# Linear attention into a sine-gated MLP on one core: a new first stage, w_in's first block in four DMAs, a re-planned order

## The chip, the cores and the metric

The kernel runs on one core of a Trainium2 chip, as one program. The core has five engines that run their own instruction streams and meet at semaphores: TensorE (PE, its weight loads shown apart as PEld), VectorE (DVE), ScalarE (ACT), GpSimd (POOL) and SyncE (SP). Data come from HBM by DMAs that POOL, ACT and SP issue. The metric is device time in microseconds (us) of one execution; a kernel's time is the median of several.

## The reference, cut to what matters

Two stages. Linear attention with a decay per head (4 batches, 8 heads, 768 tokens, head size 64), in blocks of tokens:

```
intra = (q_b k_b^T * Dmask) v_b          Dmask[i,j] = lam_h^(i-j) for i >= j, else 0
out_b = intra + (q_b * lam^(pos+1)) S    S: the carried state of the head, 64 x 64
S     = lam^block * S + (k_b * lam^(block-1-pos))^T v_b
```

Its output, laid out as x [3072 tokens, 512], goes through

```
h = x @ w_in            w_in  [512, 2048]
g = h + sin(alpha*h)^2 / alpha
y = g @ w_out           w_out [2048, 512], y is float32
```

## The kernel before, in words

**Tiling.** The reference's block of 64 tokens is computed in chunks of 128 tokens (the recurrence allows any length). There are 6 chunks t = 0..5, and chunk t of all 4 batches makes one group g = t of 512 rows for the MLP. Everything is bf16 for TensorE with float32 sums in eight PSUM banks, which the code names by number.

**The MLP of a group.** For each of 16 blocks f of 128 hidden columns: `hidden` (L311, four matmuls that sum over the 512 inputs; word h), `sine` on ACT (L316; s), a square on ACT (L322; q) or on VectorE (L324; Q), and `finish` on VectorE (L331; t), which frees the bank. Then `project` (L338; u): for each batch m, four parts of four matmuls each over w_out's four blocks; `store` (o) evicts on ACT and writes out.

**The attention of chunks 1 to 5.** Raw k and q are loaded (r, R), q is scaled by powers of lambda on POOL (z, L250), both are turned by VectorE's transpose (k, j; L226), scores F come from TensorE (L235), are masked on VectorE (m, L241), then O (L281 and L290) and its eviction x into `xt`. K, S, B and C keep the state: keys scaled on POOL (d, L246), K on TensorE (L260), S and its bf16 copy (C: on POOL, L273).

**The order.** `ORDER` is one list of words for everything after chunk 0. A word is a step, its indices and, after a colon, its banks. The loop near the end of the kernel issues the words in turn; each engine executes its own instructions in that order, so a word that waits holds up all that follows on its engine. All loads with a cast to bf16 are issued by POOL, in order with POOL's arithmetic. I and W are the loads of w_in's and w_out's blocks of 512.

**The first chunk**, which the change rewrites, stands ahead of `ORDER` and is written out by hand. POOL issues nat_k for both batch pairs, q for batches 2 and 3, then v for both pairs (`load_nat`, L131), with small tables between: an identity (masks.py), `pos_row` (L159), the token columns `pcol` (L164), a triangle (L173), `ptab` (L182); then `load_w_in(0)` (L139, two DMAs, one for each half of the partitions). SP loads q of batches 0 and 1 in float32. ACT takes Ln of lambda (L186) from `lam_bc`, which a DMA has spread over 128 partitions (L111), and Exp of it with `pcol` or `pos_row` as scales (`power`, L198, and `powers`, L209). VectorE scales q (`scale_q`, L410) and makes the mask C0 (L212). `turn0` turns k and q by TensorE, one head of 64 columns for each transpose (L379), and copies the turned heads out of PSUM on ACT (L383) or VectorE (L385). `scores0` (L391, mask L395) and `outs0` (L401; into `xt` on ACT, L405, for batches 0 and 1 and on VectorE, L407, for 2 and 3) end it. Between them stand spare matmuls on a tile of ones, `spin` (L364): 10 at the start, then 1, 1, 4 and 2, results unused. The first hidden block, h0.0, needs all four batches in `xt` and both halves of w_in's block 0.

**POOL's loads wait for each other.** The compiled program deals POOL's DMAs out to eight semaphores in turn, so a DMA waits until the one eight places ahead of it has landed. In the kernel before, POOL's DMAs are, in order: k, k, q, v, v, w_in 0 (two), w_in 1 (two), w_out 0, w_in 2 (two), w_in 3 (two), then four of raw k. POOL's first key scaling (d0.0) stands between the two pairs w_in 2 and w_in 3; the second (d0.1) stands after raw k.

Of the kernel before, what the change touches and what calls it, by code (L numbers as in the profile page):

```python
# [16 lines left out]
I1 W0 I2 d0.0 I3 h0.0:4 r1 h0.1:5 s0.0 d0.1 h0.2:7 s0.1 h0.3:2 s0.2 h0.4:3 q0.2 Q0.0 t0.0 s0.3 h0.5:6 s0.4 Q0.1  # L17
t0.1 h0.6:0 q0.3 q0.4 t0.2 h0.7:1 R1 s0.5 t0.3 s0.6 K0:45 t0.4 q0.5 u0.0.0:7 Q0.6 s0.7 t0.5 h0.8:2 S0.0 t0.6
S0.1 h0.9:3 Q0.7 C0.0 s0.8 t0.7 C0.1 h0.10:6 s0.9 Q0.8 h0.11:4 t0.8 s0.10 W1 Q0.9 u0.1.0:0 q0.10 W2 t0.9 s0.11
h0.12:5 v1 t0.10 q0.11 k1.0 h0.13:1 s0.12 h0.14:2 q0.12 t0.11 s0.13 W3 t0.12 h0.15:3 s0.14 z1.0 k1.1 u0.2.0:6  # L20
# [3 lines left out]
h1.2:1 q1.0 k2.1 s1.1 F2.0:2306 s1.2 t1.0 h1.3:4 q1.1 m2.0.0 n2 q1.2 h1.4:7 t1.1 s1.3 t1.2 h1.5:2 s1.4 P1.3  # L24
h1.6:5 q1.4 m2.0.1 r3 s1.5 h1.7:1 t1.3 s1.6 t1.4 h1.8:3 q1.5 m2.0.2 q1.6 u1.0.0:4 s1.7 t1.5 d1.0 s1.8 h1.9:7
t1.6 q1.7 m2.0.3 h1.10:0 q1.8 t1.7 d1.1 s1.9 h1.11:2 t1.8 s1.10 h1.12:5 j2.1 q1.9 q1.10 d2.0 K1:61 t1.9 s1.11
h1.13:3 s1.12 t1.10 q1.11 S1.0 h1.14:7 d2.1 q1.12 S1.1 u1.0.1 B1.0 t1.11 B1.1 h1.15:0 s1.13 t1.12 R3 s1.14 k3.0
K2:61 q1.13 u1.1.0:2 q1.14 S2.0 s1.15 u1.0.2 t1.13 v3 B2.0 t1.14 u1.1.1 q1.15 S2.1 F2.1:5637 t1.15 B2.1 u1.1.2
n3 m2.1.0 u1.0.3 m2.1.1 z3.0 m2.1.2 u1.1.3 o1.0 m2.1.3 u1.2.0:1 o1.1 k3.1 z3.1 O2:0563 j3.0 u1.3.0:4 x2.0 j3.1
x2.1 u1.2.1 x2.2 x2.3 F3.0:7205 h2.0:6 m3.0.0 m3.0.1 h2.1:3 s2.0 m3.0.2 h2.2:7 q2.0 m3.0.3 s2.1 t2.0 h2.3:2 d3.0  # L30
s2.2 u1.3.1 q2.1 q2.2 t2.1 h2.4:0 s2.3 d3.1 t2.2 h2.5:5 q2.3 s2.4 t2.3 h2.6:6 s2.5 r4 q2.4 K3:37 q2.5 t2.4
h2.7:2 s2.6 t2.5 h2.8:0 q2.6 S3.0 R4 s2.7 h2.9:5 t2.6 B3.0 h2.10:3 s2.8 Q2.7 t2.7 s2.9 h2.11:6 S3.1 v4 q2.8 q2.9
u1.2.2 t2.8 B3.1 t2.9 h2.12:2 s2.10 k4.0 s2.11 u1.3.2 n4 q2.10 k4.1 u1.2.3 q2.11 s2.12 u1.3.3 t2.10 o1.2 z4.0
t2.11 q2.12 F3.1:7053 o1.3 t2.12 u2.0.0:1 m3.1.0 h2.13:6 z4.1 m3.1.1 u2.0.1 m3.1.2 s2.13 m3.1.3 h2.14:4 q2.13
j4.0 O3:2705 s2.14 t2.13 q2.14 j4.1 d4.0 u2.0.2 x3.0 x3.1 t2.14 h2.15:3 x3.2 x3.3 F4.0:6274 d4.1 s2.15 h3.0:0
m4.0.0 q2.15 m4.0.1 h3.1:5 s3.0 t2.15 q3.0 K4:62 m4.0.2 s3.1 u2.0.3 t3.0 q3.1 m4.0.3 h3.2:3 o2.0 t3.1 u2.1.0:7
# [21 lines left out]
def kernel(  # L58
# [51 lines left out]
    lam_bc = consts.tile([P, H], FP32, name="lam_bc")  # L110
    A.dma_start(out=lam_bc[:], in_=lam.partition_broadcast(P))  # L111
# [25 lines left out]
    def load_w_in(i):  # L137
        for n in range(NQ):
            G.dma_start(out=w_in_sb[i][half[n]], in_=moe_w_in[n * 256:(n + 1) * 256, i * 512:(i + 1) * 512].rearrange(  # L139
                "(c p) g -> p c g", p=D))  # L140
# [27 lines left out]
    token_column(2, 1, 1)  # L168
    fill = consts.tile([P, 512], BF16, name="fill")
    V.memset(fill[:], 1.0)  # L170
    tri = consts.tile([P, T], FP32, name="tri")
# [11 lines left out]
    load_w_in(0)  # L183

    lnlam = consts.tile([P, H], FP32, name="lnlam")
    A.activation(out=lnlam[:], in_=lam_bc[:], func=ACTF.Ln)  # L186
# [161 lines left out]
    def project_halves(g, m):  # L348
        for n in range(2):
# [9 lines left out]
            nc.sync.dma_start(out=out[row:row + T, cols], in_=o_sb[:, 0:DM // 2])  # L359

    def spin(n, home=0):
        ps = bank("spare", home)
        for _ in range(n):
            nc.tensor.matmul(out=ps[:], lhsT=fill[:, 0:P], rhs=fill[:], start=True, stop=True)  # L364
# [154 lines left out]
```

## Time and profile before

| | us |
|---|---|
| median of 3 runs | 212.56 (210.99 to 212.8) |
| the profiled execution's own time | 212.1 |
| its span in the profile | 210.4 |
| TensorE busy | 199.4 (95%) |
| ACT busy | 149.8 (71%) |
| VectorE busy | 132.3 (63%) |
| POOL busy | 99.0 (47%) |
| TensorE's first hidden matmul starts | 19.45 |

The span is that of the recorded instructions; 1.7 us of the execution lie around it. Times in rows of the timeline count from the start of the span: a row has start, duration, engine, line, operation and tiles, the count, and in brackets the idle time before it and what ended it. "PEclk" is the share of TensorE's full clock that was granted.

### The profile page before, as it was taken

The page shows a single profiled execution, that of the slowest core. Times are in us where ns is not written, and L with a number is a line of the kernel's source. Part 1 is how long each engine was busy: PE and PEld are TensorE (multiplying, and loading weights), DVE is VectorE, ACT ScalarE, POOL GpSimd, SP SyncE. Part 2 cuts the span into 40 slices and gives each one's busy share as a digit, 9 for nine tenths or more (in the row PEclk, how much of TensorE's full clock was granted, in tenths as well). Part 3 has the DMA queues.
Part 4 walks back from the last instruction along what each step waited for, and adds up shares of the span by engine and source line. Part 5 has one row for each costly group of instructions (what it writes and reads, how often), then busy time and mean ns, then how long its engine had stood idle before and what let it go on. Part 6 is the DMA issues. An engine that isn't in the chain of part 4 may idle for free.

```text
span 210.4 us, 4948 instructions
## 1 busy us (share of the span) xinstructions
PE 199.4 (95%) x2051; PEld 96.8 (46%) x2051; DVE 132.3 (63%) x198; ACT 149.8 (71%) x260; POOL 99.0 (47%) x114
## 2 busy tenths in 40 slices
PE   7565999999999999999999999999999999999993
PEld 2242344445444454444544544544444444444452
DVE  3883579971899996599979779615552503445400
ACT  4680699505799936998798986569975955889531
POOL 7995589578999995899793600000000000000000
PEclk9999799999999999999999999999999999999999
DMA  5999999999999799399989911000111020100022
GB/s 106 154 157 205 205 193 139 159 192 213 231 153 158 78 149 179 38 154 155 158 96 189 75 50 51 35 18 3 50 50 50 0 103 37 64 21 29 3 102 97
DMA packets 68518, 22.61 MB, mean 107 GB/s; under 512 B 50944, under 2 KB 65552, under 8 KB 68496
## 3 DMA queue, kind: packets, MB, share of 16 engines
q0 software_dynamic: 62640, 15.47, 81.5%
q1 hardware_dynamic: 5680, 6.82, 9.3%
q8 instruction: 16, 0.26, 0.5%
q14 instruction: 6, 0.05, 0.1%
q10 hardware_dynamic: 176, 0.01, 0.0%
HBM read 31.47 MB, written 6.29 MB: 179 GB/s over the span
## 4 chain that ended last, share of the span: by engine, by line
PE 89%; DMA 4%; POOL 4%; issue 1%; ACT 0%; POOLq 0%; ACTq 0%
PE hps L311 41%; PE ops L338 39%; DMA w_in<-in_moe_w_in_dram 4%; PE F_ps L235 3%; PE O_ps L290 2%; PE hps L353 2%; PE O_ps L281 2%; PE KV_ps L260 2%; POOL nat_v L131 1%; POOL nat_k L131 1%; POOL raw_q L131 1%; POOL w_in L139 0%; POOL ptab L182 0%; ACT o_sb L357 0%; POOL pcol L164 0%
## 5 line engine op out<-in xcount | busy, mean ns | idle before, releaser
L331 DVE SCALAR_TENSOR_TENSOR gall<-s,r_sb,hps 128x512 bf16<-128x512 bf16 x96 | 69.1, 738 | 47.3 <-ACT s L322 37.4
L311 PE MATMUL hps<-xt,w_in 128*128 128x512 bf16 x384 | 93.6, 384 | 2.1 <-DMA w_in<-in_moe_w_in_dram 2.1
L338 PE MATMUL ops<-w_out,gall 128*128 128x512 bf16 x368 | 89.2, 379 | 0.0
L316 ACT ACTIVATE s_sb<-hps,alpha_sb 128x512 bf16<-128x512 f32 x96 | 64.2, 693 | 25.8 <-PE hps L311 25.6
L311 PEld LDWEIGHTS <-w_in 128*128 128x128 bf16 x384 | 37.5, 99 | 48.3 <-issue 5.3
L322 ACT ACTIVATE s<-s_sb 128x512 bf16<-128x512 bf16 x88 | 54.1, 639 | 1.6
L338 PEld LDWEIGHTS <-gall 128*128 128x128 bf16 x368 | 34.7, 98 | 41.4 <-issue 0.2
L241 DVE TENSOR_TENSOR STm<-F_ps,C 128x512 bf16<-128x512 f32 x40 | 25.4, 680 | 4.4 <-PE F_ps L235 4.2
L344 ACT COPY o_sb<-ops 128x512 f32<-128x512 f32 x23 | 13.5, 592 | 19.0 <-PE ops L338 17.7
L246 POOL TENSOR_TENSOR nat_k<-nat_k,R 128x1024 bf16<-128x1024 bf16 x10 | 18.9, 1920 | 4.8 <-DMA nat_k<-in_k_dram 4.7
L250 POOL TENSOR_TENSOR raw_q<-raw_q,Rraw 128x1024 bf16<-128x1024 bf16 x10 | 18.9, 1919 | 3.4 <-DMA raw_q<-in_q_dram 3.4
L124 POOL DMA_DIRECT2D raw_k<-in_k_dram x20 | 11.7, 597 | 6.2 <-DMA w_out<-in_moe_w_out_dram 3.6
L226 DVE STREAM_TRANSPOSE turned_q<-raw_q 128x512 f32<-128x512 f32 x10 | 11.0, 1100 | 5.3 <-POOL raw_q L250 5.3
L131 POOL DMA_DIRECT2D nat_v<-in_v_dram x12 | 14.0, 1173 | 0.2 <-PE ops L338 0.2
L124 POOL DMA_DIRECT2D raw_q<-in_q_dram x20 | 11.6, 592 | 3.0 <-DVE turned_q L226 2.3
L300 ACT CAST xt<-O_ps 128x512 bf16<-128x512 f32 x20 | 10.3, 600 | 2.9 <-PE O_ps L290 2.4
L131 POOL DMA_DIRECT2D nat_k<-in_k_dram x10 | 11.8, 1189 | 0.8 <-POOLq L503 0.8
L226 DVE STREAM_TRANSPOSE turned_k<-raw_k 128x512 f32<-128x512 f32 x10 | 10.6, 1112 | 0.0
L364 PE MATMUL spare<-fill 128*128 128x512 bf16 x18 | 6.9, 521 | 1.5 <-DVE fill L170 1.5
L235 PEld LDWEIGHTS <-turned_k 32*128 32x128 bf16 x320 | 4.8, 92 | 4.3 <-issue 3.4
L235 PE MATMUL F_ps<-turned_q,turned_k 32*128 32x128 bf16 x320 | 6.5, 215 | 0.0
L324 DVE TENSOR_TENSOR s<-s_sb 128x512 bf16<-128x512 bf16 x7 | 3.2, 455 | 4.6 <-ACT s_sb L316 4.6
(65 smaller groups left out, 92.6 us busy)
## 6 DMA issues: line engine op xcount, KB each, us to landing
out_dram<-o_sb SPq DMA_DIRECT2D x23, 256.0 KB, 2.0
nat_v<-in_v_dram POOLq DMA_DIRECT2D x12, 256.0 KB, 7.7
nat_k<-in_k_dram POOLq DMA_DIRECT2D x10, 256.0 KB, 7.8
raw_k<-in_k_dram POOLq DMA_DIRECT2D x20, 128.0 KB, 6.2
raw_q<-in_q_dram POOLq DMA_DIRECT2D x20, 128.0 KB, 5.4
w_in<-in_moe_w_in_dram POOLq DMA_DIRECT2D x8, 256.0 KB, 10.6
w_out<-in_moe_w_out_dram POOLq DMA_DIRECT2D x4, 512.0 KB, 10.4
raw_q<-in_q_dram SPq DMA_DIRECT2D x2, 256.0 KB, 4.7
```

The costliest lines, as they stand in the source:

```text
L124: (eng or G).dma_start(out=dst[quad[a], bs].rearrange("t b n r d -> t (b n) (r d)"), in_=src[t, a])
L131: G.dma_start(out=nat[nm, t][:, bs].rearrange("p b h e -> p (b h) e"), in_=SRC[nm][bs, :, t * T:(t + 1) * T, :].rearrange("b h p e -> p (b ...
L226: V.transpose(out=dst.rearrange("p (x t r) -> p x r t", r=R, t=32), in_=src.rearrange("p (x r d) -> p x r d", r=R, d=32))
L235: nc.tensor.matmul(out=F[a][:, u, n, :], lhsT=KQ["k", t][quad[a], 2 * pr + u, n, :, e], rhs=KQ["q", t][quad[a], 2 * pr + u, n, :, e], star ...
L241: V.tensor_tensor(out=st[t, pr][:, a], in0=att["F", pr][a], in1=C0[:, a].unsqueeze(1).broadcast_to([P, 2, NQ, T]), op=ALU.mult)
L246: G.tensor_tensor(out=kd, in0=kd, in1=R128[:].unsqueeze(1).unsqueeze(3).broadcast_to([P, 2, H, D]), op=ALU.mult)
L250: G.tensor_tensor(out=qs, in0=qs, in1=Rraw[:].rearrange("p n r -> p (n r)").unsqueeze(1).unsqueeze(3).broadcast_to([P, 2, NQ * R, D]), op= ...
L311: nc.tensor.matmul(out=hps[g, f][:], lhsT=w_in_sb[f // 4][:, c, (f % 4) * P:(f % 4 + 1) * P], rhs=xt[g][:, c, :], start=(c == 0), stop=(c ...
L316: A.activation(out=s_of[g, f][:], in_=hps[g, f][:], func=ACTF.Sin, scale=alpha_sb[:, f:f + 1])
L322: A.activation(out=s2_of[g, f][:], in_=s_sb[:], func=ACTF.Square)
L331: V.scalar_tensor_tensor(out=gall[g][:, f, :], in0=s2_of.pop((g, f))[:], scalar=r_sb[:, f:f + 1], in1=hps.pop((g, f))[:], op0=ALU.mult, op ...
L338: nc.tensor.matmul(out=ops[g, m][:], lhsT=gall[g][:, f, m * P:(m + 1) * P], rhs=w_out_sb[part][:, f % 4, :], start=(f == 0), stop=(f == NF ...
```

## The change

- lambda is loaded as one row of one partition, and eight float32 transposes of TensorE (a broadcast row against a 1x1 tile of one) spread it over 128 partitions into a PSUM bank, from which ACT takes the Ln.
- The spare matmuls are 3 ahead of those transposes and 7 behind them, then 1 after the third turn of keys and 1 at the end: 12 in place of 18.
- The two token columns that NE and Rq use are made before the identity, not after the load of q.
- `turn0` turns two heads (128 columns) with each transpose; scores, mask and outputs of the first chunk index the new layout.
- `load_w_in(0, 2)` loads w_in's first block in four DMAs: columns 0 to 255 for each half of the partitions, then columns 256 to 511.
- `ORDER` is a new list. Its first words differ most: POOL's words become I1 W0 d0.0 I2 d0.1 I3 r1, and K0 stands after the third hidden block, where it stood after the eighth.

```diff
 ORDER = """
-I1 W0 I2 d0.0 I3 h0.0:4 r1 h0.1:5 s0.0 d0.1 h0.2:7 s0.1 h0.3:2 s0.2 h0.4:3 q0.2 Q0.0 t0.0 s0.3 h0.5:6 s0.4 Q0.1
-t0.1 h0.6:0 q0.3 q0.4 t0.2 h0.7:1 R1 s0.5 t0.3 s0.6 K0:45 t0.4 q0.5 u0.0.0:7 Q0.6 s0.7 t0.5 h0.8:2 S0.0 t0.6
...
-q0.13 q0.14 t0.13 u0.3.0:4 s0.15 t0.14 z1.1 q0.15 j1.0 u0.0.1 t0.15 u0.1.1 j1.1 F1.0:5123 u0.2.1 R2 m1.0.0
-m1.0.1 u0.0.2 m1.0.2 u0.1.2 m1.0.3 r2 u0.3.1 F1.1:5123 u0.2.2 m1.1.0 m1.1.1 u0.3.2 m1.1.2 m1.1.3 u0.0.3 v2
-O1:5123 o0.0 u0.1.3 x1.0 z2.0 x1.1 u0.2.3 x1.2 x1.3 u0.3.3 o0.1 z2.1 j2.0 o0.2 h1.0:7 o0.3 k2.0 h1.1:5 s1.0 n1
+I1 W0 d0.0 I2 h0.0:2 d0.1 h0.1:4 s0.0 h0.2:5 s0.1 Q0.0 I3 t0.0 K0:73 s0.2 Q0.1 h0.3:6 S0.0 r1 t0.1 q0.2 C0.0
+h0.4:0 s0.3 t0.2 S0.1 h0.5:1 q0.3 h0.6:2 C0.1 s0.4 t0.3 s0.5 h0.7:7 R1 q0.4 u0.0.0:4 q0.5 t0.4 s0.6 u0.1.0:5
...
+q0.13 z1.0 u0.3.0:1 q0.14 t0.13 s0.15 t0.14 q0.15 z1.1 j1.0 u0.0.1 t0.15 u0.1.1 j1.1 F1.0:2736 R2 u0.2.1 m1.0.0
+m1.0.1 u0.0.2 m1.0.2 u0.1.2 m1.0.3 r2 F1.1:2736 u0.3.1 m1.1.0 m1.1.1 u0.2.2 m1.1.2 u0.3.2 m1.1.3 O1:2736 v2
+u0.0.3 x1.0 x1.1 u0.1.3 x1.2 x1.3 u0.2.3 z2.0 o0.0 o0.1 h1.0:2 o0.2 h1.1:7 s1.0 z2.1 j2.0 h1.2:3 q1.0 k2.0 s1.1
...
 """
-    lam_bc = consts.tile([P, H], FP32, name="lam_bc")
-    A.dma_start(out=lam_bc[:], in_=lam.partition_broadcast(P))
+    lam_row = consts.tile([1, H], FP32, name="lam_row")
+    A.dma_start(out=lam_row[:], in_=lam.partition_broadcast(1))
...
-    def load_w_in(i):
-        for n in range(NQ):
-            G.dma_start(out=w_in_sb[i][half[n]], in_=moe_w_in[n * 256:(n + 1) * 256, i * 512:(i + 1) * 512].rearrange(
-                "(c p) g -> p c g", p=D))
+    def load_w_in(i, parts=1):
+        w = 512 // parts
+        for j in range(parts):
+            for n in range(NQ):
+                G.dma_start(out=w_in_sb[i][half[n], :, j * w:(j + 1) * w], in_=moe_w_in[
+                    n * 256:(n + 1) * 256, i * 512 + j * w:i * 512 + (j + 1) * w].rearrange("(c p) g -> p c g", p=D))
...
     load_nat(0, "k", 1)
+    pcol = consts.tile([P, 3], FP32, name="pcol")
+
+    def token_column(n, base, step):
+        G.iota(out=pcol[:, n:n + 1], pattern=[[0, 1]], base=base, channel_multiplier=step,
+               allow_small_or_imprecise_dtypes=True)
+
+    token_column(0, -1, -1)
+    token_column(2, 1, 1)
     iden = consts.tile([P, P], BF16, name="iden")
...
     load_nat(0, "q", 1)
-    pcol = consts.tile([P, 3], FP32, name="pcol")
...
-    token_column(0, -1, -1)
-    token_column(2, 1, 1)
...
+    one = consts.tile([1, 1], FP32, name="one")
+    V.memset(one[:], 1.0)
...
-    load_w_in(0)
-
+    load_w_in(0, 2)
+    spin(3, 3)
     lnlam = consts.tile([P, H], FP32, name="lnlam")
-    A.activation(out=lnlam[:], in_=lam_bc[:], func=ACTF.Ln)
+    lam_ps = bank("lam_ps", 2)
+    for h in range(H):
+        nc.tensor.transpose(out=lam_ps[:, h:h + 1], in_=lam_row[:, h:h + 1].broadcast_to([1, P]), identity=one[:])
+    spin(7, 3)
+    A.activation(out=lnlam[:], in_=lam_ps[:, 0:H], func=ACTF.Ln)
...
-                for a in range(NA):
-                    for hq in range(NQ):
-                        nc.tensor.transpose(out=ps[half[hq], u, a, :], in_=nat[nm, 0][:, b[u], 4 * hq + a, :],
-                                            identity=iden[:])
+                for c in range(NDC):
+                    nc.tensor.transpose(out=ps[:, u, c, :], in_=nat[nm, 0][:, b[u], 2 * c:2 * c + 2, :], identity=iden[:])
...
-    spin(10, 3)
     powers()
...
-    spin(1, 3)
     scores0(0, (2, 7))
     power(R128, 1)
-    spin(1, 3)
     scores0(1, (4, 5))
     turn0("k", ((2, 3), 6, A))
-    spin(4, 3)
+    spin(1, 3)
...
     outs0(3, 0)
-    spin(2, 2)
+    spin(1, 2)
```

(`scores0`, its mask and `outs0` keep their number of instructions and their sizes; only the indices follow the new layout.)

More of the change, by code (lines that the diff above doesn't have):

```diff
@@ L27 @@
[L27 to L36, printed above, removed]
@@ L359, in project_halves @@
             nc.sync.dma_start(out=out[row:row + T, cols], in_=o_sb[:, 0:DM // 2])
[L361 to L364, printed above, removed]
     by_half, st0 = {}, {}
```

88 lines of the change are left out of this document (52 added, 36 removed).

## The prediction

> **What bounds the kernel now.** I read the page first (busy shares, the chain that ended last), then TensorE's waits, then the timeline of the first 50 us.
>
> ```profile
> PE 199.4 (95%) x2051; PEld 96.8 (46%) x2051; DVE 132.3 (63%) x198; ACT 149.8 (71%) x260; POOL 99.0 (47%) x114
> ...
> PE 89%; DMA 4%; POOL 4%; issue 1%; ACT 0%; POOLq 0%; ACTq 0%
> ```
>
> TensorE is busy nearly always and makes 89% of the chain; DMA and POOL are in it only at the beginning. Its waits say where:
>
> ```profile
> PE hps L311 <- DMA w_in<-in_moe_w_in_dram: 2.1, 1, 2.1
> PE spare L364 <- DVE fill L170: 1.5, 1, 1.5
> PE O_ps L401 <- DMA nat_v<-in_v_dram: 1.1, 1, 1.1
> ```
>
> All waits of TensorE that are longer than 0.6 us stand before 19.45 us. From there it runs almost without a gap, so a microsecond won before 19.45 is won at the end if nothing later gives it back. The early timeline, POOL's and TensorE's rows:
>
> ```profile
> 9.66 2.48 POOL L139 DMA_DIRECT2D w_in<-in_moe_w_in_dram  x4
> ...
> 13.87 0.62 POOL L139 DMA_DIRECT2D w_in<-in_moe_w_in_dram  x1 [0.34 <-PE F_ps L391]
> ...
> 15.74 0.47 PE L401 MATMUL O_ps<-STm,nat_v 128*64 128x128 bf16 x9 [1.10 <-DMA nat_v<-in_v_dram]
> 16.27 1.29 DVE L407 TENSOR_TENSOR xt<-O_ps,Etab 128x512 bf16<-128x512 f32 x2
> ...
> 17.35 0.61 POOL L139 DMA_DIRECT2D w_in<-in_moe_w_in_dram  x1 [0.29 <-DMA w_in<-in_moe_w_in_dram]
> ...
> 19.45 8.75 PE L311 MATMUL hps<-xt,w_in 128*128 128x512 bf16 x32 [2.13 <-DMA w_in<-in_moe_w_in_dram]
> 19.65 0.60 POOL L124 DMA_DIRECT2D raw_k<-in_k_dram  x1 [1.69 <-DMA w_in<-in_moe_w_in_dram]
> ...
> 24.44 0.58 POOL L124 DMA_DIRECT2D raw_k<-in_k_dram  x1 [2.09 <-DMA w_out<-in_moe_w_out_dram]
> ```
>
> Two clocks lead to h0.0. The data: the last v lands at 15.74, the last two batches of `xt` are ready at 16.27 + 1.29 = 17.56. The weights: since a POOL DMA waits for the one eight places ahead, the rows give landings. The one at 17.35 (14th) waited for w_in 0's first half (6th), the one at 19.65 (15th) for its second half, the one at 24.44 for w_out 0. So `xt` waits 1.9 us for w_in's second half. There is a second loss, in the clock (columns: busy, count, granted clock):
>
> ```profile
> 19.00:20.00 1.00, 0.55 (x3) 1.00 1.26 209
> 20.00:21.00 1.00, 1.00 (x5) 0.60 1.23 206
> 21.00:22.00 1.00, 1.00 (x4) 0.50 1.24 206
> 22.00:23.00 1.00, 1.00 (x4) 0.50 1.24 204
> 23.00:24.00 1.00, 1.00 (x5) 0.70 1.24 205
> ```
>
> Soon after the idle 17.3 to 19.45 the clock is halved, on dense work: 0.4 + 0.5 + 0.5 + 0.3 = 1.7 us lost.
>
> **w_in 0 in four DMAs.** Each of the four brings 128 KB in pieces of 256 columns, the shape of a raw k load (256 pieces as well). Their landings, each asked alone (the first and the last of four):
>
> ```profile
> raw_k<-in_k_dram POOLq DMA_DIRECT2D x1, 128.0 KB, 10.0
> raw_k<-in_k_dram POOLq DMA_DIRECT2D x1, 128.0 KB, 7.3
> ```
>
> 19.65 + 10.0 = 29.65 and 24.44 + 7.3 = 31.74: three DMAs in 2.09, 0.70 each. Behind the v at 15.74 the first pair, which h0.0 and h0.1 need, lands at 15.74 + 1.40 = 17.1. Upper bound: all of block 0 before, 19.4. I take 17.1 to 17.4 (the same bytes landed by 17.35 before). Then `xt` decides: h0.0 starts at about 17.6, 1.85 earlier. The second pair I leave where the whole block landed, 19.5 (early bound 15.74 + 2.8 = 18.5). Price on POOL: two more issues of 0.62.
>
> **POOL's new order.** Six w_in DMAs from 9.66 take 3.7 us, to 13.4; w_out 0 waits for the first v (13.87, the row above, is a DMA that waited for the same one) and goes to 14.7; d0.0 (1.9) to 16.6, w_in 2 to 17.9, d0.1 to 19.8, w_in 3 to 21.0. K0 behind h0.2 needs d0.1 at 19.8 and is ready by then. w_in 3's second DMA goes out at 20.4, 3.1 us later than before (17.35), but half of w_in 1, w_out 0 and w_in 2 then still lie ahead of it, 1.25 MB at the 204 GB/s of the windows above, some 6 us, so its landing hardly moves.
>
> **The rest of the first chunk.**
>
> ```profile
> 0.81 0.44 ACTq L111 DMA_DIRECT2D lam_bc<-in_lam_dram  x1
> ...
> 3.94 0.21 ACT L186 ACTIVATE lnlam<-lam_bc 128x8 f32<-128x8 f32 x1 [0.91 <-DMA lam_bc<-in_lam_dram]
> ...
> 5.93 0.30 ACT L198 ACTIVATE NE<-lnlam,pcol 128x8 f32<-128x8 f32 x1 [0.41 <-POOL pcol L164]
> ...
> 7.66 1.22 DVE L212 TENSOR_TENSOR C<-tri,NE 128x1024 f32<-128x1024 f32 x1
> ...
> 8.20 0.41 PE L379 MATMUL T_ps<-iden,nat_k 128*64 128x128 bf16 x8 [2.22 <-DMA nat_k<-in_k_dram]
> ...
> 11.09 1.04 PE L364 MATMUL spare<-fill 128*128 128x512 bf16 x4
> ...
> 12.23 0.20 PE L434 MATMUL a_ps<-idf,alpha_fp 16*128 16x16 f32 x1
> ```
>
> and, grouped (busy, mean ns), with the fastest landing of the page:
>
> ```profile
> L395 DVE TENSOR_TENSOR STm<-F_ps,C 128x512 bf16<-128x512 f32 x8 | 5.0, 684 | 0.3 <-PE F_ps L391 0.2
> ...
> L410 DVE TENSOR_TENSOR raw_q<-raw_q,Rq 128x512 bf16<-128x512 f32 x2 | 1.3, 688 | 0.4 <-ACT Rq L198 0.4
> ...
> L385 DVE COPY turned_q<-T_ps 128x512 bf16<-128x512 bf16 x3 | 1.3, 425 | 0.6 <-PE T_ps L379 0.6
> ```
>
> ```profile
> out_dram<-o_sb SPq DMA_DIRECT2D x23, 256.0 KB, 2.0
> ```
>
> Eight small float32 transposes: the nearest row is a_ps, 0.20 each, 1.6 us in all (0.05 each as the bf16 ones, 0.4; 0.5 each on a slow clock, 4.0). lambda's one row lands between 2.8 (issue at 0.81 and 2.0) and 3.9, as the 128 rows did. So Ln starts at 3.2 to 7.9; I take 5.2, 1.3 late. NE loses its wait for `pcol` (0.41), so it is 0.9 late, and the mask C0 ends near 9.8 in place of 8.88. The turns save 32 of 64 transposes, 32 x 0.05 = 1.6 us if a wider one costs no more, nothing if it costs double. Fewer spares in front of the q turns save 3 x 0.26 = 0.8. Late mask, fewer turns and fewer spares all stand ahead of the v that lands at 15.74: I cost them together at nothing. The cover has about 1 us on VectorE; a mask later than that moves `xt` one for one. Behind that v stand the same 16 matmuls and two 0.65 us multiplies.
>
> **The sum to the seventh block.** h0.0 and h0.1 take 2 x 0.865 at full clock: 17.6 to 19.3. h0.2 starts at 19.5; six blocks and K0 (0.6) end at 25.3. Before, eight blocks and K0 ended at 28.2 + 0.6 = 28.8. TensorE is 3.5 us ahead: 1.85 from the start, 1.7 from the clock that now has no idle stretch before it, less some waiting.
>
> **What gives some of it back.** Group 0 also has to pass ACT, POOL and VectorE:
>
> ```profile
> 20.66 0.69 ACT L316 ACTIVATE s_sb<-hps,alpha_sb 128x512 bf16<-128x512 f32 x1 [4.78 <-PE hps L311]
> ...
> 39.16 0.63 ACT L322 ACTIVATE s<-s_sb 128x512 bf16<-128x512 bf16 x1
> ```
>
> ```profile
> 29.31 0.58 POOL L124 DMA_DIRECT2D raw_q<-in_q_dram  x1 [0.67 <-DMA w_in<-in_moe_w_in_dram]
> 30.26 1.36 POOL L273 CAST Sb<-S 128x512 bf16<-128x512 f32 x2 [0.38 <-ACT S L267]
> ...
> 36.15 3.80 POOL L250 TENSOR_TENSOR raw_q<-raw_q,Rraw 128x1024 bf16<-128x1024 bf16 x2
> ```
>
> ```profile
> 40.94 1.07 DVE L226 STREAM_TRANSPOSE turned_q<-raw_q 128x512 f32<-128x512 f32 x1
> 41.86 2.45 DVE L241 TENSOR_TENSOR STm<-F_ps,C 128x512 bf16<-128x512 f32 x4
> ...
> 48.56 0.76 PE L281 MATMUL O_ps<-turned_q,Sb 32*64 32x128 bf16 x64
> ```
>
> ACT needed 19.1 us from the first sine to the last square, some 1.9 of it waiting on the half-clocked TensorE; from 18.8 that ends near 37, about 3 us earlier. POOL's last raw q still waits for w_in 3 (29.3); the two casts that came next are done before it now, so z1.0 starts 1.36 + 0.38 earlier, 34.5, and z1.1 ends at 38.3. VectorE then turns q (1.07, to 39.4) and masks F1.0 (2.45, to 41.9). F1.1 uses F1.0's banks, in both orders, and starts at 42.0. TensorE gets there at 41.3 by the sum above and waits 0.7. Three projections (0.86 each) later, and just as VectorE's next four masks end, O1 starts at 45.2. Before it was 48.56, with one projection more ahead of it: 47.7 on equal terms. **The lead is 2.5 us.** Behind O1 I let it stand: POOL is ahead by as much, and TensorE's work is the same.
>
> The profiled execution took 212.1 us, 210.4 of span and 1.7 around it; it lies 0.5 below the median of the runs. 212.1 - 2.5 = 209.6; I say **209.7**.
>
> **The rivals.**
>
> *Full lead.* Second pair at 18.5 and a shorter mask chain: 3.5 us, 208.6. Against it: POOL's z1.1, which nothing in the diff moves below 38.
>
> *The clock falls earlier.* Eighteen spares become twelve, and in the stretch from 8.2 to 17.6 only short matmuls are left with idle between them. Before, a 3.4 us stretch with about 1.25 us of work (16.8 to 20.2) was enough to halve the clock. I count about 2 us of work in each such stretch of the new one, so it should hold, with little to spare. If it doesn't: 32 output matmuls at half clock put `xt` 0.8 later, and 3.4 us of dense blocks lose 1.7; the lead falls from 3.3 to 0.8, **211.3**. The Trainium skill ("TensorE: Matmul & The Clock Gate", Part 1) has the clock return to half after an idle window of about 3.4 us; this trace differs, since 2.1 us of idle sufficed. The same page (Part 4) says that transposes don't count as busy work for this gate; by that the turns would not hold the clock and this rival would be the forecast, which no row here decides.
>
> *The split doesn't do it.* The four DMAs finish together, as w_in 0's second half did at 19.4 though its bytes alone ask for 1.4 us after 17.35. Then h0.0 starts at 19.4 and the clock falls as before: 211.9.
>
> *Slower: lambda by TensorE.* Everything of the first chunk hangs on Ln, and TensorE's queue has the spares behind the transposes. From Ln to `xt` the chain without slack is 1.6 to NE (5.93 - 0.41 - 3.94), 0.6 for NE and Rq, 1.3 scaling, 1.2 mask, 0.8 turned q (two copies), 2.5 for four of L395, 0.4 for the third copy, 2.5 for the other four, 1.3 into `xt`: 12.2 us. It passes the old 19.45 when Ln starts after 7.2, that is with transposes above 0.4 us each. At 0.6 each, from 3.9, Ln starts at 8.7 and `xt` is ready at 20.9, or at 21.7 with the output matmuls at half clock after so much idle time; with dense blocks cold as before that is 212.1 + 2.3 = 214.4, and 215.8 at 0.77 each. The a_ps row speaks against it.
>
> **How the numbers follow.** Forecast 0.50 (208.8 to 210.5), full lead 0.12, cold clock 0.20, split without effect 0.08, slower 0.10. About 1% (2.1 us) is what a measurement here can tell from no change; faster by more than that means below 210.4: nearly all of the forecast and the full lead, none of the others, 0.60. Slower by over 1% means above 214.7: 0.06, rather more than half of the last case. Within: 0.34. The range takes in full lead and cold clock and leaves out the far ends: 208.2 to 211.8.
>
> **What would show it.** Right: h0.0 at 17.4 to 17.8, waiting for `xt`; granted clock 1.00 from 17 to 24; a short wait ahead of h0.2; F1.1 near 42, O1 near 45. Wrong: Ln after 6; a clock below 1.00 between 10 and 20; h0.0 still released by a w_in DMA after 19; TensorE waiting on VectorE or POOL anywhere after O1, which would show the new order giving back what the start won.

## The result, and the profile after

The changed kernel takes **210.38 us** (median of 22 runs, 209.29 to 212.47) against **211.66 us** for the kernel before (22 runs beside them, 210.91 to 213.82). The ratio is 0.994 with a 95% interval of 0.9915 to 0.9965: faster by 1.28 us, about half of what the sum had promised. The first profile of the changed kernel fell on the slowest of these executions (212.47), so what follows is a later one of the same kernel, 209.58 us with a span of 207.9, near its fast end.

From the page of the changed kernel (busy time of each engine, granted clock in 40 slices, the chain that ended last):

```profile
PE 198.7 (96%) x2021; PEld 97.2 (47%) x2021; DVE 133.2 (64%) x201; ACT 148.1 (71%) x258; POOL 101.2 (49%) x116
...
PEclk9996999999999999999999999999999999999999
...
PE 79%; DVE 12%; ACT 4%; issue 2%; DMA 2%; DVEq 0%; ACTq 0%
```

TensorE is busy for about as long as before, 198.7 us against 199.4. What changed is the chain: POOL has gone from it, and the DMAs' share has fallen from 4% to 2%. VectorE's 12% is some 24 us: 7 in the first chunk, 12 between 17 and 45 us and 4 between 51 and 58. TensorE hardly waits in the later two stretches, so there VectorE's work and TensorE's have become about equally long. The "6" in the fourth slice is a clock that fell again. TensorE's waits (total, times, longest):

```profile
PE spare L192 <- DVE one L174: 1.5, 1, 1.5
PE O_ps L410 <- DMA nat_v<-in_v_dram: 1.2, 1, 1.2
PE hps L325 <- DVE xt L416: 0.8, 1, 0.8
```

The 2.1 us for w_in is gone. The first hidden block now waits for `xt`, as forecast. The timeline, rows of ACT, TensorE, VectorE and POOL:

```profile
2.92 1.01 PE L198 MATMUL lam_ps<-one,lam_row 1*128 1x1 f32 x8
...
3.96 0.18 ACT L200 ACTIVATE lnlam<-lam_ps 128x8 f32<-128x8 f32 x1 [0.94 <-PE lam_ps L198]
...
14.79 0.88 PE L410 MATMUL O_ps<-STm,nat_v 128*64 128x128 bf16 x16 [1.24 <-DMA nat_v<-in_v_dram]
15.31 1.29 DVE L416 TENSOR_TENSOR xt<-O_ps,Etab 128x512 bf16<-128x512 f32 x2
...
16.75 4.44 PE L325 MATMUL hps<-xt,w_in 128*128 128x512 bf16 x12 [0.76 <-DVE xt L416]
...
33.98 3.76 POOL L264 TENSOR_TENSOR raw_q<-raw_q,Rraw 128x1024 bf16<-128x1024 bf16 x2 [0.19 <-DMA raw_q<-in_q_dram]
...
39.62 2.47 DVE L255 TENSOR_TENSOR STm<-F_ps,C 128x512 bf16<-128x512 f32 x4
...
42.08 0.68 PE L249 MATMUL F_ps<-turned_q,turned_k 32*128 32x128 bf16 x32
...
45.38 0.76 PE L295 MATMUL O_ps<-turned_q,Sb 32*64 32x128 bf16 x64
```

And TensorE by stretches (busy and count, granted clock, DMA engines busy, GB/s):

```profile
16.00:18.00 2.00, 1.25 (x4) 0.76 1.16 167
18.00:20.00 2.00, 2.00 (x6) 0.50 1.24 205
20.00:22.00 2.00, 2.00 (x71) 0.89 1.24 206
```

F1.1 starts at 42.08 (forecast 42.0) and O1 at 45.38 (forecast 45.2). That hit is partly luck: h0.0 starts 0.85 us earlier than forecast, because the last v landed by 14.79 and not at 15.74, and then the halved clock that was to be gone takes 0.24 x 2 + 0.5 x 2 + 0.11 x 2 = 1.7 us of dense work (the first 12 matmuls take 4.44 us, and 2.75 at full clock in a kernel below).

### The profile page after: what moved, and what is told of

The parts are those of the page before. It is cut to its first block, busy times and chain, and to the rows that moved or that the text cites. A ratio compares the mean times of both kernels' runs of the same rounds, so it can differ in the third digit from the quotient of the medians.

```text
span 210.8 us, 4860 instructions
## 1 busy us (share of the span) xinstructions
PE 197.1 (94%) x1992; PEld 97.7 (46%) x2021; DVE 135.7 (64%) x201; ACT 148.1 (70%) x258; POOL 100.8 (48%) x116
## 4 chain that ended last, share of the span: by engine, by line
PE 74%; DMA 11%; DVE 5%; POOL 4%; ACT 2%; issue 2%; DVEq 0%; ACTq 0%; POOLq 0%
PE ops L352 35%; PE hps L325 29%; DMA w_in<-in_moe_w_in_dram 4%; DMA w_out<-in_moe_w_out_dram 4%; DMA nat_k<-in_k_dram 3%; PE F_ps L249 3%; PE O_ps L304 2%; DVE gall L345 2%; POOL nat_k L260 2%; DVE STm L255 2%; PE hps L367 2%; PE O_ps L295 2%; POOL w_in L141 1%; DVE S L283 1%; PE T_ps L387 1%
## 5 line engine op out<-in xcount | busy, mean ns | idle before, releaser
L325 PE MATMUL hps<-xt,w_in 128*128 128x512 bf16 x372 | 90.9, 379 | 2.0 <-issue 0.7
L352 PE MATMUL ops<-w_out,gall 128*128 128x512 bf16 x352 | 88.1, 382 | 4.0 <-DMA w_out<-in_moe_w_out_dram 2.4
L325 PEld LDWEIGHTS <-w_in 128*128 128x128 bf16 x384 | 36.7, 98 | 46.0 <-issue 2.2
L336 ACT ACTIVATE s<-s_sb 128x512 bf16<-128x512 bf16 x86 | 52.9, 638 | 1.6
L264 POOL TENSOR_TENSOR raw_q<-raw_q,Rraw 128x1024 bf16<-128x1024 bf16 x10 | 18.9, 1919 | 4.0 <-DMA raw_q<-in_q_dram 4.0
L338 DVE TENSOR_TENSOR s<-s_sb 128x512 bf16<-128x512 bf16 x9 | 5.9, 657 | 2.4 <-ACT s_sb L330 2.4
L192 PE MATMUL spare<-fill 128*128 128x512 bf16 x11 | 5.0, 607 | 1.5 <-DVE one L174 1.5
```

The lines of the kernel that those rows point to most:

```text
L264: G.tensor_tensor(out=qs, in0=qs, in1=Rraw[:].rearrange("p n r -> p (n r)").unsqueeze(1).unsqueeze(3).broadcast_to([P, 2, NQ * R, D]), op= ...
L325: nc.tensor.matmul(out=hps[g, f][:], lhsT=w_in_sb[f // 4][:, c, (f % 4) * P:(f % 4 + 1) * P], rhs=xt[g][:, c, :], start=(c == 0), stop=(c ...
L336: A.activation(out=s2_of[g, f][:], in_=s_sb[:], func=ACTF.Square)
L352: nc.tensor.matmul(out=ops[g, m][:], lhsT=gall[g][:, f, m * P:(m + 1) * P], rhs=w_out_sb[part][:, f % 4, :], start=(f == 0), stop=(f == NF ...
```

## The experiments

Three things were open. Was the first profile of the kernel before typical, with its late half of w_in and its cold start? Which part carries the gain: the new list of words, the split of w_in, lambda's row, the wider transposes, the spares? And where did the other half of the forecast go? Ratios are to the kernel before, run beside each experiment on the same chip (its medians there were 211.58 to 211.67), with 95% intervals.

**The kernel before, once more**, and **the changed kernel, once more**. No edits.

> The kernel before once more, for a second profile. Theory B (the profile that the forecast started from was an execution with two costs that most don't have: w_in 0's second half 1 to 1.5 us late, and a whole stretch of half clock on dense blocks): the first hidden block starts at 17.8 to 18.8 in place of 19.45 and less than 1.7 us of clock is lost after it; O1 near 47.5 to 48.1, time 211.2 to 211.8. Rival O: 19.4 and O1 at 48.5 again, so that the lead of the first chunk is as large as forecast and is lost later in the changed kernel.

> The changed kernel once more, for a second profile. Theory W (the lead of the start is spent waiting for w_out block 1 at u0.0.1): the first projection of part 1 again starts when that DMA lands, at 37.5 to 38.5 us, after an idle stretch of TensorE of 1.5 to 2.4 us, whatever the time; the clock falls behind it in some executions and not in others, which makes the spread of 209.3 to 212.5. Rival O (the first profile was an odd execution): no wait above 0.5 us at u0.0.1, O1 near 45.5, time near 209.5.

Before: 211.63 us, 0.9996 [0.9975, 1.0017]. Changed: 210.32 us, 0.9945 [0.992, 0.9969]; its profile is the one above. Theory W is not borne out by it: TensorE doesn't wait at u0.0.1, and O1 starts at 45.38, as rival O has it. The timeline of the kernel before, in its second profile (211.88 us, span 210.1):

```profile
18.55 7.07 PE L311 MATMUL hps<-xt,w_in 128*128 128x512 bf16 x32 [0.37 <-DVE xt L407]
...
47.06 1.02 PE L338 MATMUL ops<-w_out,gall 128*128 128x512 bf16 x4 [1.18 <-DMA w_out<-in_moe_w_out_dram]
48.02 0.76 PE L281 MATMUL O_ps<-turned_q,Sb 32*64 32x128 bf16 x64
```

and its stretches:

```profile
8.00:12.00 4.00, 4.00 (x62) 0.57 2.96 153
...
20.00:24.00 4.00, 4.00 (x21) 1.00 1.24 206
```

Here h0.0 starts 0.9 us earlier than in the first profile, it waits for `xt` and not for w_in, and eight blocks run at full clock, 7.07 us against 8.75. So neither of the forecast's two losses is a fixed property of the kernel before. And yet the execution is as long: O1 starts at 48.02, only 0.54 earlier than the 48.56 of the first profile. A lead of 2.6 us behind the eight blocks (K0 starts at 25.55 against 28.14) shrinks to some 1.8 by F1.1, and most of that goes in the projection ahead of O1 (u0.0.3), which waits 1.18 us for w_out 3. That was to be read in the first profile too, in rows that the forecast passed over (POOL's and TensorE's timeline of the kernel before):

```profile
45.74 2.89 PE L338 MATMUL ops<-w_out,gall 128*128 128x512 bf16 x12
...
47.85 0.58 POOL L124 DMA_DIRECT2D raw_k<-in_k_dram  x1 [1.48 <-DMA w_out<-in_moe_w_out_dram]
```

POOL's raw k at 47.85 is the eighth DMA behind w_out 3, so w_out 3 landed just ahead of that. The last four matmuls of the 45.74 row, u0.0.3, cannot have started much earlier. TensorE came there at the same moment, so no wait was on show. A start won before that point would have stopped there.

**Only the new list of words**, on the kernel before.

```diff
 ORDER = """
-I1 W0 I2 d0.0 I3 h0.0:4 r1 h0.1:5 s0.0 d0.1 h0.2:7 ...
+I1 W0 d0.0 I2 h0.0:2 d0.1 h0.1:4 s0.0 h0.2:5 s0.1 Q0.0 I3 t0.0 K0:73 ...
```

> The kernel before with the new order list alone. Theory D: the first hidden block still starts near 19.4, nothing arrives earlier at O1 than TensorE's work allows, O1 near 47.5 (one projection more is left behind it); time 211.3 to 212, the same as before. Rival N (the order alone carries the gain, by keys scaled earlier and u0.0.3 behind O1): time 210 to 210.8.

210.67 us, 0.9967 [0.9947, 0.9986]. The timeline of its profile (210.13 us, span 208.4), rows of TensorE and POOL:

```profile
17.83 2.75 PE L311 MATMUL hps<-xt,w_in 128*128 128x512 bf16 x12 [0.77 <-DMA w_in<-in_moe_w_in_dram]
...
44.90 0.76 PE L281 MATMUL O_ps<-turned_q,Sb 32*64 32x128 bf16 x64
...
46.49 0.58 POOL L124 DMA_DIRECT2D raw_k<-in_k_dram  x1 [2.73 <-DMA w_out<-in_moe_w_out_dram]
...
49.51 3.77 POOL L250 TENSOR_TENSOR raw_q<-raw_q,Rraw 128x1024 bf16<-128x1024 bf16 x2
...
57.51 1.89 PE L311 MATMUL hps<-xt,w_in 128*128 128x512 bf16 x8 [0.64 <-DVE gall L331]
```

The list alone is measurably faster, by 0.7 us (the ratio) to 0.9 (the medians), although the first chunk is the old one and h0.0 still waits for w_in. That is rival N, not theory D. O1 no longer stands behind u0.0.3 and starts at 44.90. Some of it is returned: at 57.51 TensorE waits 0.64 us for VectorE's `gall`. The chain that ended last leads from there back to w_out 3 once more. POOL's fourth raw k waits 2.73 us for it, behind that stand the loads of v and the scaling of q (z2.0), and VectorE's turns and `gall` follow them. So the new list takes w_out 3 off TensorE's own way and leaves it on POOL's.

**Only the new first chunk**, with the old list.

```diff
 ORDER = """
-I1 W0 d0.0 I2 h0.0:2 d0.1 h0.1:4 s0.0 h0.2:5 s0.1 Q0.0 I3 t0.0 K0:73 ...
+I1 W0 I2 d0.0 I3 h0.0:4 r1 h0.1:5 s0.0 d0.1 h0.2:7 ...
```

> The changed first chunk and its four DMAs, with the order list of the kernel before. Theory D (in the old order u0.0.3 stands ahead of O1 and needs w_out block 3, which lands at 46 to 47.7 us whatever TensorE does, so a lead of the start is given back there): h0.0 near 16.8, then TensorE waits 1 to 2.5 us for w_out 3 or for d0.1 before O1, O1 at 47.5 to 48.5; time 210.9 to 211.6, within 0.4% of the kernel before. Rival S (the start alone carries the gain): O1 near 46, time 209.8 to 210.5 as the changed kernel.

211.19 us, 0.998 [0.996, 1.0001]. Its timeline:

```profile
17.22 3.61 PE L325 MATMUL hps<-xt,w_in 128*128 128x512 bf16 x16 [0.61 <-DVE xt L416]
...
26.16 0.42 PE L274 MATMUL KV_ps<-nat_v,nat_k 128*32 128x64 bf16 x32 [1.22 <-POOL nat_k L260]
...
47.02 1.02 PE L352 MATMUL ops<-w_out,gall 128*128 128x512 bf16 x4 [0.76 <-DMA w_out<-in_moe_w_out_dram]
47.97 0.76 PE L295 MATMUL O_ps<-turned_q,Sb 32*64 32x128 bf16 x64
```

h0.0 starts 1.33 us earlier than in the second profile of before, at full clock, and O1 0.05 earlier. The lead goes into K0, which waits 1.22 us for POOL's second key scaling (d0.1 stands behind raw k in the old list), and into waits for w_out. Theory D holds. This is the clearest answer to where a good start goes without the new list. The profiles say the same by the time from h0.0 to O1. With the old list it is 29.1 us where h0.0 starts at 19.45 (1.7 of it the halved clock) and 30.8 at full clock where it starts at 17.22 or 17.44: O1 stays at 48.0 to 48.6. With the new list it is 27.1 in the profile with that list alone and 28.6 in the changed kernel's above, 1.7 of which is the clock; the projection that now stands behind O1 explains 0.86 of the difference. So with the new list O1 moves with h0.0, unless w_out 1 comes late (below), and with the old one it doesn't. The two halves together:

| | old first chunk | new first chunk |
|---|---|---|
| old list | 211.65 | 211.19 (0.998) |
| new list | 210.67 (0.9967) | 210.32 (0.9945) |

They add up: 0.33% and 0.20% against 0.55% for both. Only the list's step is clear of 1 by its interval, the first chunk's isn't. That the list is the larger one agrees with the mechanism; the two intervals overlap, so the order of size is not shown by the times alone.

**Lambda's row and TensorE's transposes alone**, on the kernel before, and **the changed kernel with lambda spread by the DMA**.

```diff
-    lam_bc = consts.tile([P, H], FP32, name="lam_bc")
-    A.dma_start(out=lam_bc[:], in_=lam.partition_broadcast(P))
+    lam_row = consts.tile([1, H], FP32, name="lam_row")
+    A.dma_start(out=lam_row[:], in_=lam.partition_broadcast(1))
...
+    spin(3, 3)
+    for h in range(H):
+        nc.tensor.transpose(out=lam_ps[:, h:h + 1], in_=lam_row[:, h:h + 1].broadcast_to([1, P]), identity=one[:])
+    spin(7, 3)
```

(the second experiment is this edit undone in the changed kernel, with the ten spares in one piece)

> The kernel before with one part of the change alone: lambda as one row, spread by TensorE between 3 and 7 spares. Theory L: first k lands at 7.1, last v at 14.6, w_in 0's second half at 18.2, so h0.0 starts at 18.3 in place of 19.45; with the idle stretch before it about as long as in the kernel before, the clock falls as often. Time 0.5 to 1.1 us below the kernel before. Rival T: no difference in the landings and none in the time.

> The changed kernel with lambda spread by the 128-row DMA again and no TensorE transposes for it (the ten spares at the start stay). Theory L (the 128 small rows of that DMA delay every other load at the start by about 1.1 us): the first k lands at 8.1 to 8.2 in place of 7.1, the last v at 15.7 in place of 14.6, h0.0 starts at 17.6 to 17.9 in place of 16.8. If theory W also holds, the end moves by less than that, 0 to 0.7 us later than the changed kernel. Rival T (k came earlier because of another part of the change): k lands at 7.1 still.

Alone: 211.31 us, 0.9986 [0.9957, 1.0015], no difference that shows. Undone: 210.85 us, 0.9959 [0.9933, 0.9985] against 0.9945 for the changed kernel, not resolved either. Both by their timelines; alone on the kernel before:

```profile
17.44 7.07 PE L323 MATMUL hps<-xt,w_in 128*128 128x512 bf16 x32 [0.39 <-DMA w_in<-in_moe_w_in_dram]
...
47.32 1.02 PE L350 MATMUL ops<-w_out,gall 128*128 128x512 bf16 x4 [2.15 <-DMA w_out<-in_moe_w_out_dram]
48.28 0.76 PE L293 MATMUL O_ps<-turned_q,Sb 32*64 32x128 bf16 x64
```

and undone in the changed kernel:

```profile
7.74 0.40 PE L384 MATMUL T_ps<-iden,nat_k 128*128 128x128 bf16 x4 [1.85 <-DMA nat_k<-in_k_dram]
...
17.79 5.08 PE L322 MATMUL hps<-xt,w_in 128*128 128x512 bf16 x12 [0.34 <-DVE xt L413]
```

The first of them starts h0.0 at 17.44 with no loss of clock and then waits 2.15 us for w_out 3: the same stop as above, more plainly. Theory L had expected 0.5 to 1.1 us and keys that land 1.1 us earlier; neither shows. Over all profiles the first turn of keys starts at 7.64 to 8.20 where lambda comes over 128 rows (four profiles, mean 7.81) and at 7.15 to 7.79 where it comes as one row (ten, mean 7.53). The means differ by 0.3 us, but the ranges overlap and the one start at 8.20 makes half of it, so that the broadcast delays the first loads is not shown. The Trainium skill ("DMA: Bandwidth & Descriptors", Issuing engines are not separate DMA queues) says that DMAs share the same 16 engines whichever engine issued them. By that ACT's row could delay POOL's keys; these starts don't decide it.

**The changed kernel with w_in 0 in two DMAs.**

```diff
-    load_w_in(0, 2)
+    load_w_in(0, 1)
```

> The changed kernel with w_in's first block in two DMAs, all else as changed. The split is worth what h0.0 waits without it: w_in 0 is whole at 17.3 to 18.5, so h0.0 starts at 17.5 to 18.6 in place of 16.8, but h0.2 does not wait any more. Theory D: the end of group 0's blocks hangs on ACT, POOL and the loads, so the time moves by 0 to 0.5 us against the changed kernel, to 210.3 to 210.9. Rival S: all of the later start shows, 0.8 to 1.7 us, 211.2 to 212.

211.12 us, 0.9996 [0.9968, 1.0024], against 0.9945 [0.992, 0.9969] with four. By the medians the split is worth some 0.8 us; the two intervals just touch, so this is at the edge of what is resolved. The time lies between theory D and rival S, nearer to S. Its timeline and its stretches:

```profile
18.63 4.44 PE L325 MATMUL hps<-xt,w_in 128*128 128x512 bf16 x12 [1.18 <-DMA w_in<-in_moe_w_in_dram]
```

```profile
16.00:20.00 4.00, 2.30 (x14) 0.89 1.20 189
20.00:24.00 4.00, 4.00 (x75) 0.69 1.23 203
```

Without the split h0.0 waits 1.18 us for w_in with `xt` ready. The clock falls as well, 0.11 x 4 + 0.31 x 4 = 1.7 us, but that much was lost with four DMAs too, so it is not the price of the missing split. Within the first chunk the split is the only part for which the times show a price, and without it no gain on the kernel before is resolved (the medians are 211.12 and 211.58).

**Is it w_out 1?** In the first profile of the changed kernel, the execution of 212.47, TensorE had waited 2.4 us for it, and O1 started at 48.39:

```profile
38.49 2.37 PE L352 MATMUL ops<-w_out,gall 128*128 128x512 bf16 x8 [2.39 <-DMA w_out<-in_moe_w_out_dram]
...
48.39 0.76 PE L295 MATMUL O_ps<-turned_q,Sb 32*64 32x128 bf16 x64
```

One kernel takes that wait away by reading block 0 in its place; the other leaves out all loads of w_out but the first and reads block 0 throughout.

```diff
-                             rhs=w_out_sb[part][:, f % 4, :],
+                             rhs=w_out_sb[0 if g == 0 and part == 1 else part][:, f % 4, :],
```

```diff
-                             rhs=w_out_sb[part][:, f % 4, :],
+                             rhs=w_out_sb[0][:, f % 4, :],
...
-        "I": load_w_in, "W": load_w_out, "r": lambda t: load_raws(t, "k"), "R": lambda t: load_raws(t, "q"),
+        "I": load_w_in, "W": lambda i: load_w_out(i) if i == 0 else None, "r": lambda t: load_raws(t, "k"), ...
```

> The changed kernel with one part changed: group 0's projections of part 1 read w_out block 0 in place of block 1, so nothing waits for block 1 until part 2's blocks; the loads and their order stay. Theory W: TensorE goes on at 36.1, F1.0 near 39, the next wait is for w_out 2 (landing near 41.4) or for VectorE; the time falls by 1 to 2.5 us against the changed kernel, to 208 to 209.5. Rival O: no change, within 0.5 us.

> The changed kernel without the loads of w_out blocks 1 to 3: every projection reads block 0, so 1.5 MB of loads and all waits for these blocks are gone, while every matmul stays. Theory D (the loads of the first 45 us decide how much of the lead survives): no wait of TensorE for a DMA after 17 us, raw q and v of chunk 1 land up to 3 us earlier, O1 at 44.5 to 45.3 in every execution; median 208.8 to 209.5 and a spread below 1.5 us. Rival P (TensorE, ACT and VectorE decide): median and spread as the changed kernel, 210.3 and 2.5 to 3 us.

Without the dependence on w_out 1: 210.48 us, 0.9951 [0.992, 0.9982], no difference that shows. Without the loads of w_out 1 to 3: 209.93 us, 0.9931 [0.9901, 0.9962], perhaps 0.4 us, not resolved; the runs still spread over 3 us (208.65 to 211.68). Theories W and D both expected more. So with the new list no large share of the median hangs on w_out, though these intervals leave room for up to about 1 us, and the spread between runs of the changed kernel doesn't come from these loads.

**The spares.** The old later spares (1, 1, 4, 2) in the changed kernel; one float32 matmul of a row of ones against lambda's row in place of the eight transposes, all later spares behind it; and that one with spares in the waits for v and `xt` as well.

```diff
     turn0("q", ((1,), 1, V))
+    spin(1, 3)
     scores0(0, (2, 7))
     power(R128, 1)
+    spin(1, 3)
...
-    spin(1, 3)
+    spin(4, 3)
...
-    spin(1, 2)
+    spin(2, 2)
```

```diff
-    one = consts.tile([1, 1], FP32, name="one")
+    one = consts.tile([1, P], FP32, name="one")
...
-    for h in range(H):
-        nc.tensor.transpose(out=lam_ps[:, h:h + 1], in_=lam_row[:, h:h + 1].broadcast_to([1, P]), identity=one[:])
-    spin(7, 3)
+    nc.tensor.matmul(out=lam_ps[:, 0:H], lhsT=one[:], rhs=lam_row[:], start=True, stop=True)
+    spin(9, 3)
```

```diff
     A.activation(out=warm[:], in_=lnlam[:, 0:1], func=ACTF.Sin)
+    spin(3, 2)
     scores0(2, (2, 7))
...
     outs0(1, 6)
+    spin(4, 1)
...
-    spin(1, 2)
+    spin(3, 2)
```

> The changed kernel with the later spare matmuls of the kernel before (1, 1, 4, 2 in place of 1, 1). Theory C (the changed first chunk leaves TensorE at half clock at the wrong time, from the eight small transposes that interrupt the first spares and from too few spares later): the early cold stretch stays, since nothing before the first turn changes, but the fall at 16 to 21 us goes; median 209.9 to 210.4, 0 to 0.4 us below the changed kernel, spread smaller. Rival F (spares cost time in front of the turns and save nothing): 210.4 to 211.

> The changed kernel with lambda spread by one float32 matmul (a row of 128 ones against the row of 8) in place of eight transposes, and 9 spares behind it in place of 7. Theory C: the hole of 1.0 us in the first spares shrinks to 0.3, so the turns of the first chunk run at full clock (four transposes in 0.22 to 0.25, not 0.43) in every execution, h0.0 starts at 16.5 to 17.0 in place of 16.8 to 18.0; median 209.5 to 210.0, 0.4 to 0.8 below the changed kernel. Rival F: the early clock does not matter, within 0.2 us of the changed kernel.

> As the one with a single matmul for lambda, and with more spares where TensorE waits in the first chunk: 3 ahead of the scores of batch 2, 4 ahead of the outputs of batch 2, 3 at the end. Theory C: full clock from 7 us through group 0, h0.0 at 16.6 to 17.0, O1 at 44.5 to 45.2; median 209.0 to 209.6, the fastest of all, spread below 1.5 us. Rival F: the spares stand in the way, h0.0 at 17.2 or later, median 210 or above.

Old spares: 210.24 us, 0.9938 [0.9911, 0.9965]; one matmul: 209.84 us, 0.9919 [0.9893, 0.9945]; one matmul and filled waits: 210.22 us, 0.9931 [0.9899, 0.9962]. First the stretches of the kernel with the old spares, then the timeline with one matmul, then timeline and stretches with the waits filled:

```profile
16.00:20.00 4.00, 3.56 (x14) 0.65 1.22 189
```

```profile
2.92 0.59 PE L197 MATMUL lam_ps<-lam_row,one 1*128 1x8 f32 x2
...
17.28 3.40 PE L324 MATMUL hps<-xt,w_in 128*128 128x512 bf16 x12 [0.58 <-DVE xt L415]
...
44.87 0.76 PE L294 MATMUL O_ps<-turned_q,Sb 32*64 32x128 bf16 x64
```

```profile
17.07 2.75 PE L324 MATMUL hps<-xt,w_in 128*128 128x512 bf16 x12 [0.36 <-DVE xt L415]
...
35.73 1.89 PE L351 MATMUL ops<-w_out,gall 128*128 128x512 bf16 x8 [0.51 <-DMA w_out<-in_moe_w_out_dram]
...
44.30 0.76 PE L294 MATMUL O_ps<-turned_q,Sb 32*64 32x128 bf16 x64
...
57.87 1.89 PE L324 MATMUL hps<-xt,w_in 128*128 128x512 bf16 x8 [0.63 <-DVE gall L344]
```

```profile
16.00:20.00 4.00, 3.64 (x49) 1.00 1.25 204
```

The clock falls in the profile with the old spares as well, so it can fall without their removal. The mean granted clock on record for every execution says more. A loss of 1.7 us is 0.8% of the span, so a mean below 0.995 means that over 1 us was lost: 22 of 32 executions of the changed kernel, 4 of 12 with the old spares, 1 of 10 with the waits filled. So the spares may well make the fall rarer, and filling the waits nearly removes it from the record. With filled waits O1 starts earlier than in any other profile (44.30), and the end doesn't follow: span less O1 is 164.0 there, against 162.5 for the changed kernel, and TensorE waits 0.63 us for `gall`. The median, 210.22, misses theory C's 209.0 to 209.6. The fastest median is that of the one matmul, inside its theory's range although h0.0 starts at 17.28 and not by 17.0; it beats the kernel before clearly, and its interval overlaps with the changed kernel's, so that it beats that one too is not shown.

## Why the prediction was right or wrong

**The base (mis-sized).** The forecast subtracted 2.5 from one execution of 212.1. That base is 0.44 above the median of 22 runs (211.66), and the gain of 2.5 is 1.22 above the measured 1.28; the two errors have opposite signs, and 209.7 is 0.7 too low. Between the two profiled executions, 212.1 and 209.58, the difference is 2.5, as forecast: one was rather slow for its kernel, the other rather fast.

**"1.85 from the start" (mis-sized).** The mechanism holds. h0.0 waits for `xt` and no longer for w_in, and a kernel without the split waits 1.18 us. But the late half of w_in in the first profile was partly that execution's: the second profile of before starts h0.0 at 18.55, waiting for `xt`. With the new list the old first chunk starts h0.0 at 17.83, and with lambda's row at 17.44. Over the three profiles of the old first chunk without the row h0.0 starts at 17.83 to 19.45 (mean 18.61), over the eight of the new one with the split and the row at 16.75 to 17.98 (mean 17.26): the gain at the start is some 1.35, and the ranges overlap.

**"1.7 from the clock that now has no idle stretch before it" (failed).** The kernel before need not lose it on dense blocks (1.00 in 20 to 24 in its second profile), and the changed kernel can: 1.7 us in the profile above, with waits of 1.24 and 0.76 us left ahead of h0.0. The mean clocks agree: below 0.995 in 62 of 104 executions of the kernel before (those beside the experiments and its own twelve) and in 22 of 32 of the changed one, so the change hasn't removed the loss. My cold-clock rival had the price on the dense blocks right and gave it too little chance. The later `xt` that it added doesn't show in that profile. Its condition, fewer spares, is not settled: the clock falls with the old ones too, if perhaps less often. The result lies between the forecast and that rival.

**"47.7 on equal terms ... TensorE's work is the same" (failed).** This step compared O1 with O1 less one projection, as if TensorE alone set it. In the old list O1 stands behind u0.0.3, which needs w_out 3, and all four profiles with that list have O1 at 47.97 to 48.56 while h0.0 starts anywhere from 17.22 to 19.45. I took the new list as neutral but for POOL's words. By the medians it is the larger part of the gain: it takes u0.0.3 from ahead of O1 and d0.1 from behind raw k. So a right number stood on a wrong cause: most of the lead that I put down to the start would have been lost in the old list.

**What gives some back (numbers held, the wait did not).** z1.0 was forecast for 34.5 and starts at 33.98; the masks end at 42.09 (forecast 41.9) and F1.1 starts at 42.08. But TensorE was to arrive at 41.3 and wait 0.7 us for the masks, and no such wait shows: it waits 0.29 us for `gall` at 38.83, inside F1.0, and then comes to F1.1 just as the masks end. "Behind O1 I let it stand" holds for this profile: span less O1 is 162.1 for the second profile of before and 162.5 for the changed kernel, which has one projection (0.86) more behind O1. No wait above 0.2 us shows on TensorE behind O1. Where O1 starts earlier it need not hold: in the kernel with the list alone (O1 at 44.90) and in that with the waits filled (44.30) span less O1 is 163.5 and 164.0, with the waits for `gall` at 57.51 and 57.87 that my last sign of being wrong had named.

**Lambda by TensorE (held, smaller).** Eight transposes took 1.01 us and not 1.6, the row landed by 2.9, and Ln started at 3.96 (forecast 5.2). The slower rival is refuted.

**The wider transposes (settled by two rows).** The forecast left open whether a wide transpose costs double. Third turn of keys, the kernel before and then the changed one:

```profile
10.52 0.64 PE L379 MATMUL T_ps<-iden,nat_k 128*64 128x128 bf16 x16
```

```profile
9.69 0.62 PE L387 MATMUL T_ps<-iden,nat_k 128*128 128x128 bf16 x8
```

Half the number takes the same time, so the turns save TensorE nothing, as the lower case of the forecast had it.

**The wait ahead of h0.2 (wrong).** It doesn't show, neither on the halved clock of the profile above nor at full clock with the waits filled, where 12 matmuls run through from 17.07 in 2.75 us, which puts h0.2 at some 18.9. So the second pair of DMAs had landed by then, nearer to the early bound of 18.5 than to 19.5. The split was not without effect, so that rival falls; full lead was not reached.

**What stays open.** Runs of the changed kernel spread over 3 us, those of either half alone over some 1 us (0.9 with the list, 1.1 with the first chunk). Taking out w_out's loads, putting the spares back and filling the waits, one at a time, left 2.2 to 3 us of it. The clock on record doesn't explain it either: the ten executions of the changed kernel with a mean of 0.997 or more run from 209.49 to 211.70.

## What to carry to other kernels

Before you credit a lead, look along the path for the next load that everything waits for, even where no wait is on show: a transfer that lands just as the engine arrives is invisible in the waits, and its landing can be read from the instruction of the queue that its semaphore released. A wait that a new order takes from one engine can live on in another's queue, as w_out 3 does on POOL here. Compare start and end on the path that the *old* order enforces, not on equal work. And take two profiles of the kernel before you subtract from one; the two losses that this forecast set out to remove, the wait for w_in and the halved clock on dense blocks, were missing in the second.

## What was not expected of the hardware

**The clock stretch moves between executions.** Seven of the fourteen profiles lose 1.7 us of granted clock in one stretch, that is some 3.4 us at half pace; one loses 6.8 (lambda by the DMA) and six lose none on record. In two executions of one kernel the stretch lay in different places: the kernel before had 0.60 and 0.50 in 20 to 23 in its first profile, and 0.57 in 8 to 12 with 1.00 in 20 to 24 in its second. The Trainium skill ("TensorE: Matmul & The Clock Gate", Part 1) says that the gate's window runs freely, so that one kernel meets it at different phases; these two profiles agree. Behind h0.0 the stretch costs 1.7 us. Early it costs less, but not nothing: the last v landed at 15.74 and 15.77 in these two profiles, and VectorE began its two multiplies into `xt` at 16.27 and, with the early stretch, at 17.12.

**The granted clock doesn't show every slow stretch.** The changed kernel without w_out 1 to 3, first its timeline, then its stretches:

```profile
7.63 0.61 PE L387 MATMUL T_ps<-iden,nat_k 128*128 128x128 bf16 x4 [0.59 <-DMA nat_k<-in_k_dram]
```

```profile
8.00:12.00 4.00, 4.00 (x40) 1.00 2.38 152
```

The four turns take 0.61 us, where they take 0.40 in the profile with lambda's DMA, and the next twelve keep the slow pace, with a granted clock of 1.00 on record. Where a stretch looks slow, compare the mean duration of like instructions as well as the clock. That this early pace is the granted clock's too, from a time before its first change on record, is likely but was not shown.

**Landing times vary by a microsecond and more.** w_in 0's second half was the last thing h0.0 waited for at 19.45 in one execution of the kernel before and not at 18.55 in another; the last v was there at 15.74 in one profile and at 14.79 in another (of the changed kernel). A sum that rests on one landing carries that much.
